# Attention and a maximum feed-forward on one core: the running maximum spread another way, the weights converted earlier, the first key sums on TensorE

## The chip, the cores and the metric

The kernel runs on one core of a Trainium2 chip. The metric is device time in microseconds (us), lower is better: three runs of the kernel before and their median, and one profiled execution with its own time. TensorE (PE) multiplies, VectorE (DVE) and ScalarE (ACT) work on SBUF and PSUM, GpSimd (POOL) on SBUF, and SyncE (SP) issues transfers. Each engine takes its instructions in order from its own queue and waits on semaphores for the others.

## The reference

Attention over 8 batches and 8 heads, 1152 keys, head size 64, with each two neighbouring queries averaged (576 queries), then a feed-forward in which a maximum over three products stands for the activation. All data is float32.

```python
q_pool = q.reshape(B, H, S // 2, 2, D).mean(axis=3)
scores = np.matmul(q_pool, k.transpose(0, 1, 3, 2)) / np.sqrt(D)
scores = scores - np.max(scores, axis=-1, keepdims=True)
attn = np.exp(scores)
attn = attn / (np.sum(attn, axis=-1, keepdims=True) + 1e-09)
x = np.matmul(attn, v).transpose(0, 2, 1, 3).reshape(B * 576, 512)
h = np.maximum(np.maximum(x @ w1, x @ w2), x @ w3)      # 768 wide
out = h @ w_out                                         # 4608 x 512
```

The weights w1, w2, w3 and w_out come as 64-bit floats.

## The kernel before, in words

**Units.** The attention is cut into 64 units, numbered d: one pair of heads of a batch and one half (288) of its queries; eight units make a batch. A unit's scores lie with the 128 keys of a block on the partitions and 2 x 288 columns (two heads), for nine blocks. `scores` makes them, `values` the rest.

- For each block PE multiplies with q split into a high and a low part (lines 542, 543, reduced float32: `F32R`), ACT copies the result out of PSUM into s (548), and DVE keeps the running maximum over the blocks in acc (554 for the first two, 557). Three blocks share one buffer "third" of `spool`, which has six: the copies of a unit wait for values and key sums of the unit two before it.
- acc still has 128 partitions to be reduced. PE transposes it in five pieces of 115 or 116 columns, three into one PSUM bank and two into another (593), DVE takes the maximum over each row (599), and PE spreads it back over all partitions by five more transposes of a broadcast operand (609). DVE subtracts it from the three thirds, in two spans of 345 and 231 columns (624), ACT takes the exponential (630).
- The sum over keys: POOL adds the nine blocks into ksum (643, 645), eight additions a unit. For units below `EARLY` = 16, PE turns ksum into columns with six one-column products (704), DVE adds EPS and inverts (714, 694), PE spreads it (719) and DVE multiplies (728). From unit 16, PE sums with a matrix of ones (687), ACT adds EPS (691), DVE inverts 288 columns (694), POOL multiplies (697).
- The value product: 18 products of 288 columns in float32 (673), two heads in two 64-wide tiles of the array; ACT copies it out (682), ACT and POOL split it into a high and a low part for the feed-forward (772, 775).

**Feed-forward.** Tokens go in nine chunks (512 each, then 448 and 576); chunk b starts when the attention of batch b is ready. 18 groups of weights (`NG`), each split into high and low, are multiplied (935), the maximum over three is formed (954, 956), split again (963, 966) and multiplied by the output weight (990). A chunk of weights is fetched from a scratch copy w_split in device memory (895).

**Conversion.** In chunk 0 each of the 18 groups, and the six tiles of the output weight, is converted from the bits of 64-bit floats (`convert`, 813 to 890): ACT rescales the high word into PSUM (835), DVE shifts (838), puts in the sign (843), isolates the power (848) and scales the low word (851), ACT takes the high part (862), and POOL (even tiles) or DVE (odd tiles, in halves of 256) subtracts (865) and adds (868). The product of chunk 0 reads the converted tile directly, and it is stored to w_split too (881). A tile is loaded when the tile two before it is done.

**Order.** Every operation is a `Step` with the engines it may run on, an assumed cost, and its predecessors. `arrange` (193) plays the steps through with these costs and, at each moment, gives an engine the ready step of lowest rank; a rank is the unit's number plus a constant of its kind (`RANK`) and for the first units a `NUDGE`. The resulting order is written out as the instruction order of the five engines. The bank pool "ff" of two PSUM banks serves the feed-forward, the sums, the conversions and, below unit 8, the value products.

Of the kernel before, what the change touches and what calls it, by code (L numbers as in the profile page):

```python
# [18 lines left out]
P = 128  # L19
# [4 lines left out]
CB = 115  # L24
DM = 512
# [11 lines left out]
    "qk": -364.0396,  # L37
    "cp": -126.5549,
    "mx": -318.2574,
    "rows": -969.9796,  # L40
    "red": -172.0313,
    "bc": -345.8464,
    "sub": 215.1752,
    "exp": 196.9402,
    "keys": -671.9276,
    "av": 14.8431,
    "xcopy": -516.1778,
    "psum": 398.4083,
    "eps": 343.2889,
    "inv": 357.0576,  # L50
    "xm": -706.0274,
    "load": 386.6538,
    "prep": 638.9001,
    "move": 1290.4425,
    "split": 283.1141,
    "ffn": -33.8173,
    "rate": 1.047,
    "mm": 49.0387,
    "fetch": 603.0832,
    "evac": -724.5554,  # L60
    "hhigh": 1228.3483,
    "hlow": -714.7034,
    "conv": 648.8915,
    "rate0": 4.5084,
    "first_qk": -97.1625,
    "first_cp": -630.79,
    "first_mx": 212.4188,
    "first_sub": 204.5779,
    "first_exp": 244.1512,
    "first_keys": -1118.9276,  # L70
    "first_av": 141.406,
    "first_xcopy": -152.0387,
    "first_psum": 65.359,
    "first_inv": 141.5566,
    "first_xm": 829.3378,
    "first_load": -197.5173,
    "first_prep": 180.1798,
    "first_move": -1436.3679,
    "first_split": 375.0794,
# [226 lines left out]
def tile_attention_ffn(  # L306
# [498 lines left out]
    def ffn(b, d):  # L805
# [108 lines left out]
        for g in range(4):  # L914
            supply(g)
# [159 lines left out]
```

## Time and profile before

| | |
|---|---|
| three runs | 1474.91, 1472.44, 1477.5 us; median 1474.91 |
| profiled execution | 1472.96 us, of which the span from the first to the last instruction is 1471.1 |
| mean granted TensorE clock | 0.978 |
| instructions | PE 8704, DVE 1441, ACT 1464, POOL 835 |
| transferred | 240.71 MB, mean 164 GB/s |

The page of the profile has the busy time of each engine, the span in 40 slices of 36.8 us (a digit is the busy share in tenths; PEclk is the granted TensorE clock in tenths), the DMA queues, the chain of waits that ended last, and the costliest groups of instructions by line. Other views: windows (busy time of each engine in stretches of the span, with instruction counts in brackets), lines (groups by line and shape: busy time, mean ns of one, then the idle time of the engine before them and what ended it), waits, and the timeline. A matmul's duration overlaps those of its neighbours, so a row of many gives less time than the sum of their durations.

### The profile page before, as it was taken

The numbers are of one execution on the slowest core, as the hardware profiler recorded it, in microseconds if no ns is written. First come the engines' busy times: TensorE is split into PE (matmuls) and PEld (weight loads), VectorE is DVE, ScalarE is ACT, GpSimd is POOL, SyncE is SP. The second block draws the span as 40 slices with busy tenths as digits, with TensorE's granted clock in tenths as the row PEclk, the third lists the DMA queues.
The fourth block names the chain that finished last, engine by engine and source line by source line (L and its number), as shares of the span: only waits on it lengthen the run. The fifth ranks groups of instructions, "written<-read, shape, count | busy, mean of one in ns | idle before, by whom it ended". The sixth has DMA issues, their size and how long they took to land.

```text
span 1471.1 us, 24704 instructions
## 1 busy us (share of the span) xinstructions
PE 1398.0 (95%) x8704; PEld 1098.5 (75%) x8704; DVE 1044.0 (71%) x1441; ACT 902.5 (61%) x1464; POOL 1079.1 (73%) x835
## 2 busy tenths in 40 slices
PE   4888999898899999999999999999999999999999
PEld 4566677675677878777777777777777777878999
DVE  3897789898877767777688778777787768861110
ACT  3776776567666666567566766666766757651211
POOL 1897975889868878679888878888787978772210
PEclk9988999998899999999999999999999999999999
DMA  6675456576456656565567556664566556414441
GB/s 181 169 203 147 122 153 207 184 206 194 118 151 185 201 155 182 168 181 148 148 192 203 152 145 191 182 182 134 163 189 184 149 148 185 144 69 162 149 161 59
DMA packets 114762, 240.71 MB, mean 164 GB/s; under 512 B 15440, under 2 KB 75216, under 8 KB 114640
## 3 DMA queue, kind: packets, MB, share of 16 engines
q1 hardware_dynamic: 114064, 238.55, 55.8%
q8 instruction: 70, 1.15, 0.3%
q10 hardware_dynamic: 576, 0.59, 0.2%
q14 instruction: 52, 0.43, 0.1%
HBM read 144.70 MB, written 18.87 MB: 111 GB/s over the span
## 4 chain that ended last, share of the span: by engine, by line
PE 75%; DVE 10%; DMA 4%; ACT 4%; issue 4%; POOL 2%; SPq 1%; ACTq 0%; DVEq 0%; POOLq 0%
PE ph L935 28%; PE pav L673 14%; PE po L990 10%; PE pqk L542 9%; PE pqk L543 8%; DVE s L624 3%; DVE acc L557 3%; DMA kraw<-in_kT_dram 2%; PE pmt L593 2%; PE psum L687 2%; PE pmb L609 2%; POOL ksum L645 1%; ACT s L548 1%; DVE w L848 1%; DVE w L843 1%
## 5 line engine op out<-in xcount | busy, mean ns | idle before, releaser
L645 POOL TENSOR_TENSOR ksum<-ksum,s 128x576 f32<-128x576 f32 x448 | 638.2, 1425 | 26.1 <-ACT s L630 3.5
L935 PE MATMUL ph<-xh,w 128*128 128x512 f32 (+2 forms) x1440 | 464.3, 376 | 2.7 <-DVE w L868 1.3
L548 ACT COPY s<-pqk 128x576 f32<-128x576 f32 x576 | 362.4, 639 | 103.4 <-PE pqk L543 97.8
L624 DVE TENSOR_TENSOR s<-s,pmb 128x693 f32<-128x693 f32 (+1 forms) x384 | 395.1, 1049 | 39.5 <-PE pmb L609 38.3
L542 PE MATMUL pqk<-qq,kc 128*128 128x288 f32 x1152 | 357.9, 326 | 56.1 <-DVE acc L557 30.7
L557 DVE TENSOR_TENSOR acc<-acc,pqk 128x576 f32<-128x576 f32 x448 | 335.3, 749 | 82.8 <-ACT s L548 78.1
L630 ACT ACTIVATE s<-s 128x693 f32<-128x693 f32 (+1 forms) x384 | 352.5, 933 | 41.9 <-DVE s L624 38.6
L543 PE MATMUL pqk<-qq,kc 128*128 128x288 f32 x1152 | 332.3, 303 | 0.0
L542 PEld LDWEIGHTS pqk<-qq,kc 128*128 128x128 f32 x1152 | 225.6, 196 | 113.7 <-DVE acc L557 44.5
L673 PE MATMUL pav<-s,v 128*64 128x288 f32 x2304 | 306.8, 418 | 1.3 <-ACT s L630 1.0
L935 PEld LDWEIGHTS ph<-xh,w 128*128 128x128 f32 x1440 | 263.1, 188 | 41.4 <-ACT xr L682 1.8
L935 PE MATMUL ph<-xl,w 128*128 128x512 f32 (+2 forms) x720 | 268.3, 373 | 0.0
L673 PEld LDWEIGHTS pav<-s,v 128*64 128x64 f32 x2304 | 165.2, 140 | 119.3 <-issue 16.6
L543 PEld LDWEIGHTS pqk<-qq,kc 128*128 128x128 f32 x1152 | 227.5, 197 | 10.4
L643 POOL TENSOR_TENSOR ksum<-s 128x576 f32<-128x576 f32 x64 | 92.0, 1437 | 107.8 <-ACT s L630 104.8
L956 DVE TENSOR_TENSOR hm<-hm,ph 128x512 f32<-128x512 f32 (+2 forms) x120 | 75.8, 631 | 126.8 <-PE ph L935 124.8
L966 POOL TENSOR_TENSOR h_lo<-hm,h_hi 128x512 fp32r<-128x512 f32 (+2 forms) x60 | 70.6, 1176 | 126.1 <-ACT h_hi L963 123.6
L935 PEld LDWEIGHTS ph<-xl,w 128*128 128x128 f32 x720 | 135.8, 189 | 11.5
L438 POOL TENSOR_TENSOR kraw<-kraw 128x1152 fp32r<-128x1152 f32 x31 | 82.8, 2670 | 63.1 <-DMA qraw<-in_qT_dram 26.6
L599 DVE TENSOR_REDUCE m<-pmt 116x3 f32<-116x384 f32 (+1 forms) x128 | 61.3, 488 | 89.9 <-PE pmt L593 89.8
L682 ACT COPY xr<-pav 128x288 f32<-128x288 f32 x64 | 25.5, 399 | 147.0 <-PE pav L673 146.9
L694 DVE RECIPROCAL rs<-rs 128x288 f32<-128x288 f32 (+1 forms) x64 | 96.5, 1507 | 17.7 <-ACT rs L691 17.3
(57 smaller groups left out, 1293.6 us busy)
## 6 DMA issues: line engine op xcount, KB each, us to landing
w<-w_split SPq DMA_DIRECT2D x144, 512.0 KB, 3.6
kc<-kraw SPq DMA_DIRECT2D x384, 96.0 KB, 2.2
qq<-qraw SPq DMA_DIRECT2D x252, 144.0 KB, 3.3
v<-in_vr_dram SPq DMA_DIRECT2D x32, 576.0 KB, 3.8
kraw<-in_kT_dram SPq DMA_DIRECT2D x31, 576.0 KB, 6.0
qraw<-in_qT_dram SPq DMA_DIRECT2D x31, 576.0 KB, 4.0
w<-in_win_dram SPq DMA_DIRECT2D x18, 512.0 KB, 5.9
w_split<-w SPq DMA_DIRECT2D x18, 512.0 KB, 5.5
```

What stands on the lines that cost most here:

```text
L542: nc.tensor.matmul(ps[:, h - hs[0], :QH], w, qq[:, 0, h], start=True, stop=False)
L543: nc.tensor.matmul(ps[:, h - hs[0], :QH], w, qq[:, 1, h], start=False, stop=True)
L548: nc.scalar.copy(o.s[kk // 3][:, kk % 3, slice(*hs)], o.ps[kk, hs][:, :, :QH])
L557: nc.vector.tensor_tensor(acc, acc, ps, op=ALU.max)
L624: nc.vector.tensor_tensor(s, s, o.pb[h][:, None, :w].broadcast_to([P, 3, w]), op=ALU.subtract)
L630: nc.scalar.activation(s, s, AF.Exp, scale=SCALE)
L643: vec[e].tensor_tensor(o.ksum, o.s[0][:, 0], x, op=ALU.add)
L645: vec[e].tensor_tensor(o.ksum, o.ksum, x, op=ALU.add)
L673: nc.tensor.matmul(o.pav[64 * h : 64 * h + 64, :QH], pr.v[:, kk, h], o.s[kk // 3][:, kk % 3, h], start=(kk == 0), stop=(kk == NK - 1),)
L694: nc.vector.reciprocal(o.rs, o.rs)
L935: nc.tensor.matmul(t.ps[:, : hi - lo], w[:, a, kk], xx[:, kk, lo:hi], start=(kk == 0 and i == 0), stop=(kk == 3 and i == 2),)
L990: nc.tensor.matmul(t.ps[:, : hi - lo], ww[:, kk, ms], hh[:, kk, lo:hi], start=(kk == 0 and i == 0), stop=(kk == 5 and i == 2),)
```

## The change

Five edits come together; the tables `RANK` and `NUDGE` have other numbers, and the order of all engines with them.

1. From unit 16 (`TURN`) the maximum goes another way. DVE reduces acc with a transposing reduction to 18 columns (`fold`), PE transposes that once (`turn`), DVE takes the maximum over four groups (`summit`: 18 x 32 values), ACT and DVE split it into a high and a low part (`m_high`, `m_low`), POOL multiplies it with a selecting pattern into a block-diagonal operand of 18 x 32 columns (`spread_out`), and PE multiplies ones by each half of it (`bcast_wide`, 288 columns in F32R). The spans are 288 and 288. The next unit's acc waits for `fold` alone.
2. In units 0 to 7 (`SUMS`) POOL adds no keys. After the values PE multiplies a 32-wide matrix of ones by all 18 half blocks, in four column tiles of the array (`columns_keys`); ACT copies the partial sums (`sums_copy`), PE adds and turns them (`sums_turn`).
3. `spool` has seven thirds, and in units 0 to 7 (`LENT`) the last third of a unit lies in one of four buffers that later hold h of the feed-forward.
4. A conversion uses whole tiles of 512: ACT rescales, DVE shifts and puts in the sign, ACT turns the low word into a float, POOL adds, ACT takes the high part, POOL subtracts. All 24 are put ahead of chunk 0, which fetches from w_split like the others.
5. `dynamic_dma_scratch_size=1024` is passed to the compiler.

```diff
+TURN = 16
+THIRDS = 7
+LENT = 8
+SUMS = 8
...
-    spool = ctx.enter_context(tc.tile_pool(name="spool", bufs=6))
+    spool = ctx.enter_context(tc.tile_pool(name="spool", bufs=THIRDS))
-    hpool = ctx.enter_context(tc.tile_pool(name="hpool", bufs=1))
+    hpool = ctx.enter_context(tc.tile_pool(name="hpool", bufs=4))
...
+        def fold(e):
+            nc.vector.tensor_reduce(
+                crest[d % 2][:, :NB],
+                o.acc.rearrange("p h q -> p (h q)").rearrange("p (t k) -> p t k", t=NB),
+                axis=AX.X, op=ALU.max, apply_transpose=True,
+            )
+        def turn(e):
+            o.pb[0] = ps_a.tile([P, 512], F32, tag="a", name=f"pmb{d}_0")
+            nc.tensor.transpose(o.pb[0][:, QH : QH + P], crest[d % 2], ident)
+        def summit(e):
+            o.top = o.pb[0][:NB, QH + P : QH + P + SQ]
+            nc.vector.tensor_reduce(
+                o.top, o.pb[0][:NB, QH : QH + P].rearrange("p (g k) -> p k g", g=4), axis=AX.X, op=ALU.max
+            )
+        def m_high(e):
+            nc.scalar.copy(parts2[d % 2][:NB], o.top)
+        def m_low(e):
+            nc.vector.tensor_tensor(parts2[d % 2][SQ : SQ + NB], o.top, parts2[d % 2][:NB], op=ALU.subtract)
+        def spread_out(e):
+            nc.gpsimd.tensor_tensor(
+                diag[d % 2][: 2 * SQ],
+                pick[:, :, None].broadcast_to([2 * SQ, NB, SQ]),
+                parts2[d % 2][:, None, :].broadcast_to([2 * SQ, NB, SQ]),
+                op=ALU.mult,
+            )
+            def bcast_wide(e, h=h):
+                if h:
+                    o.pb[h] = ps_b.tile([P, 512], F32, tag="b", name=f"pmb{d}_{h}")
+                half = diag[d % 2][:, NB // 2 * h : NB // 2 * h + NB // 2]
+                nc.tensor.matmul(o.pb[h][:, :QH], wide, half.rearrange("p t k -> p (t k)"), start=True, stop=True)
...
-        for kk in range(1, NK):
+        for kk in range(1, NK) if d >= SUMS else ():
...
+        def columns_keys(e):
+            o.psm = ps_ff.tile([P, 512], F32, tag="ff", name=f"psum{d}")
+            for kk in range(NK):
+                for h in range(2):
+                    t = 2 * h + kk % 2
+                    nc.tensor.matmul(
+                        o.psm[32 * t : 32 * t + 32, :QH], ones[:, :32], o.s[kk // 3][:, kk % 3, h],
+                        start=kk < 2, stop=kk >= NK - 2, tile_position=(0, 32 * t),
+                    )
+        def sums_copy(e):
+            nc.scalar.copy(o.kt, o.psm[:, :QH])
+        def sums_turn(e):
+            for i in range(3):
+                nc.tensor.matmul(
+                    o.psm[:96, QH + 2 * i : QH + 2 * i + 2], o.kt[:, 96 * i : 96 * i + 96], sel, start=True, stop=True
+                )
...
-                a = cstep([act(m)], rebias, [loaded] + gone, take="ff")
+                a = cstep([act(m)], rebias, [loaded], take="ff")
                 a = cstep([dve(m)], shift, [a])
-                a = cstep([dve(m)], sign, [a])
-                c = cstep([("act", 0.09 + m / 1200)], high, [a])
-                a = cstep([dve(m)], power, [a])
-                a = cstep([dve(m)], rest, [a], give=None if wide else "ff")
-                end = dve(m) if wide else pool(m)
-                c = cstep([end], low, [c, a])
-                return cstep([end], total, [c, a], give="ff" if wide else None)
+                a = cstep([dve(m)], sign, [a], give="ff")
+                c = cstep([act(m)], units_of, [loaded])
+                a = cstep([pool(m)], carry, [a, c])
+                c = cstep([("act", 0.09 + m / 1200)], high, [a] + gone + highs[-1:])
+                highs.append(c)
+                return cstep([pool(m)], low, [c, a])
...
         def supply(g):
-            if b:
-                fetch(g)
-            else:
-                convert(g)
-                fetched[g] = converted[g]
+            fetch(g)
...
+        if b == 0:
+            for g in range(NG + 6):
+                convert(g)
```

More of the change, by code (lines that the diff above doesn't have):

```diff
@@ L24 @@
 CB = 115
+SQ = 32
+NB = 18
+TURN = 16
 DM = 512
@@ L36 @@
 RANK = {
[L37 to L79, printed above, removed]
+    "qk": -1610.0615,
+    "cp": -180.1672,
+    "mx": -1253.2067,
+    "rows": -786.0194,
+    "turn": -1110.3828,
+    "top": 469.0602,
+    "diag": -189.5205,
+    "red": 77.8083,
+    "bc": -879.861,
+    "sub": 3840.475,
+    "exp": 984.6769,
+    "keys": -2399.561,
+    "av": 683.8571,
+    "xcopy": -1571.289,
+    "psum": 782.1931,
+    "eps": 214.1172,
+    "inv": 1557.6025,
+    "xm": -150.8782,
+    "load": -1024.6367,
+    "prep": 2386.9581,
+    "move": 1089.3258,
+    "split": -86.6507,
+    "ffn": 707.8881,
+    "rate": 5.1716,
+    "mm": 974.547,
+    "fetch": 157.873,
+    "evac": -1776.9799,
+    "hhigh": 675.1121,
+    "hlow": -1456.4392,
+    "conv": 1545.6563,
+    "rate0": 0.2612,
+    "first_qk": -105.5392,
+    "first_cp": 492.9138,
+    "first_mx": 996.4585,
+    "first_sub": 621.8249,
+    "first_exp": 463.1478,
+    "first_keys": -3171.6001,
+    "first_av": -465.3423,
+    "first_xcopy": 820.1949,
+    "first_psum": 3176.8613,
+    "first_inv": 117.4318,
+    "first_xm": -1228.9986,
+    "first_load": -1485.6615,
+    "first_prep": 53.3922,
+    "first_move": -618.3481,
+    "first_split": 1939.7866,
 }
 NUDGE = {
[81 rows of a table removed]
[90 rows of a table added]
 }
@@ L340, in tile_attention_ffn, with blank @@
     nc.vector.memset(eps, EPS)
+    sel = cpool.tile([P, 2], F32, name="sel")
+    nc.vector.tensor_tensor(sel, ident[:, ::64], ident[:, 32::64], op=ALU.add)
+    wide = cpool.tile([P, P], F32R, name="wide")
+    nc.vector.memset(wide.bitcast(F32), 1.0)
+    pick = cpool.tile([2 * SQ, NB], F32, name="pick")
+    crest = [cpool.tile([P, P], F32, name=f"crest{i}") for i in range(2)]
+    parts2 = [cpool.tile([2 * SQ, SQ], F32R, name=f"parts{i}") for i in range(2)]
+    diag = [cpool.tile([P, NB, SQ], F32R, name=f"diag{i}") for i in range(2)]
+    def blank():
+        for i in range(2):
+            rows = slice(SQ * i, SQ * i + SQ)
+            nc.vector.tensor_copy(pick[rows], ident[rows, SQ * i : SQ * i + NB])
+            nc.vector.memset(crest[i], 0.0)
+            nc.vector.memset(parts2[i].bitcast(F32), 0.0)
+            nc.vector.memset(diag[i].bitcast(F32), 0.0)
     wo_hi = cpool.tile([P, 6, DM], F32R, name="wo_hi")
@@ L515, in heads @@
         )
+    blanks = step("top", TURN - 4, [("dve", 3.2)], lambda e: blank(), [])
     units = {}
+    homes = [[], []]
     uses, last, finish, scaled, spreads = [[], []], [None], {}, {}, {}
@@ L522, in scores @@
         o = units[d] = Job()
-        o.n, o.half = n, half
+        o.n, o.half, o.d = n, half, d
         pr = pairs[n]
@@ L546, in copy @@
                     if kk % 3 == 0:
-                        o.s[kk // 3] = spool.tile([P, 3, 2, QH], F32, tag="s", name=f"s{d}_{kk // 3}")
+                        if d < LENT and kk == 6:
+                            s = hpool.tile([P, 3, NQ], F32, tag="t", name=f"s{d}_2")
+                            o.s[2] = s.rearrange("p k (h q) -> p k h q", h=2)
+                        else:
+                            o.s[kk // 3] = spool.tile([P, 3, 2, QH], F32, tag="s", name=f"s{d}_{kk // 3}")
                     nc.scalar.copy(o.s[kk // 3][:, kk % 3, slice(*hs)], o.ps[kk, hs][:, :, :QH])
@@ L571, in scores @@
                 after = [m]
-                if kk % 3 == 0 and old2:
-                    after += [old2.avs[kk + 2], old2.sums[kk + 1]]
+                if kk % 3 == 0:
+                    lent = d < LENT and kk == 6
+                    seq = homes[lent]
+                    past = len(seq) - (4 if lent else THIRDS)
+                    if past >= 0:
+                        was, last_kk = seq[past]
+                        after += [was.avs[last_kk], was.sums[last_kk - 1] if was.sums else chain[was.d]]
+                    seq.append((o, kk + 2))
                 c = x = step("cp", r, [act(n * QH)], copy, after + copies[-1:])
@@ L576, in scores @@
                 if kk:
-                    after = [c] + ([copies[0]] + (old.rows if old else []) if kk == 1 else [tops[-1]])
+                    after = [c] + ([copies[0]] + (old.accread if old else []) if kk == 1 else [tops[-1]])
                     x = step("mx", r, [dve(n * QH)], top, after, give="ff" if apart else None)
@@ L585, in scores @@
         pools = (ps_a, ps_b)
-        for h, (x0, x1) in enumerate([(0, 3 * CB), (3 * CB, 2 * QH)]):
+        late = d >= TURN
+        spans = [(0, QH), (QH, 2 * QH)] if late else [(0, 3 * CB), (3 * CB, 2 * QH)]
+        free_a = old.subs[0] if old else []
+        bc = {}
+        def fold(e):
+            nc.vector.tensor_reduce(
+                crest[d % 2][:, :NB],
+                o.acc.rearrange("p h q -> p (h q)").rearrange("p (t k) -> p t k", t=NB),
+                axis=AX.X,
+                op=ALU.max,
+                apply_transpose=True,
+            )
[18 more added lines that the diff above has]
+            )
+        if late:
+            x = step("red", d, [("dve", 0.775)], fold, [tops[-1], blanks, getattr(old2, "turned", None)])
+            o.accread = [x]
+            x = o.turned = step("turn", d, [pe(150)], turn, [x] + free_a)
+            x = step("top", d, [("dve", 0.25)], summit, [x])
+            y = step("top", d, [("act", 0.2)], m_high, [x] + getattr(old2, "full", []))
+            x = step("top", d, [("dve", 0.17)], m_low, [x, y] + getattr(old2, "full", []))
+            full = step("diag", d, [("pool", 1.16)], spread_out, [x, y] + getattr(old2, "bcs", []))
+            o.full = [full]
+            o.bcs = []
+        for h, (x0, x1) in enumerate(spans):
             nb, w = 3 - h, x1 - x0
@@ L613, in bcast @@
                     )
-            gone = xout[d - 1] if d > SPLIT and h else None
-            x = step("rows", d + 0.1 * h, [pe(133 * nb)], rows, [tops[-1], gone] + (old.subs[h] if old else []))
-            o.rows.append(x)
-            x = step("red", d, [("dve", 0.067 + nb * 0.133)], reduce, [x])
-            b = step("bc", d + 0.1 * h, [pe(89 + 99 * nb)], bcast, [x])
+            def bcast_wide(e, h=h):
[3 more added lines that the diff above has]
+                nc.tensor.matmul(
+                    o.pb[h][:, :QH], wide, half.rearrange("p t k -> p (t k)"), start=True, stop=True
+                )
+            gone = xout[d - 1] if d > SPLIT and h else None
+            if late:
+                b = step("bc", d + 0.1 * h, [pe(145)], bcast_wide, [full, gone] + (old.subs[1] if h else []), cols=QH)
+                o.bcs.append(b)
+            else:
+                x = step(
+                    "rows", d + 0.1 * h, [pe(133 * nb)], rows, [tops[-1], gone] + (old.subs[h] if old else [])
+                )
+                o.rows.append(x)
+                x = step("red", d, [("dve", 0.067 + nb * 0.133)], reduce, [x])
+                b = step("bc", d + 0.1 * h, [pe(89 + 99 * nb)], bcast, [x])
             for i in range(3):
@@ L635, in scores @@
                 o.exps[i, h] = step("exp", r, [("act", 0.109 + w / 400)], exp, [x])
+        if not late:
+            o.accread = o.rows
         o.sums = []
-        for kk in range(1, NK):
+        for kk in range(1, NK) if d >= SUMS else ():
             def key(e, kk=kk):
@@ L710, in columns @@
                     )
+        def columns_keys(e):
[4 more added lines that the diff above has]
+                    nc.tensor.matmul(
+                        o.psm[32 * t : 32 * t + 32, :QH],
+                        ones[:, :32],
+                        o.s[kk // 3][:, kk % 3, h],
+                        start=kk < 2,
+                        stop=kk >= NK - 2,
+                        tile_position=(0, 32 * t),
+                    )
+        def sums_copy(e):
+            o.kt = small.tile([P, QH], F32, tag="kt", name=f"kt{d}", bufs=1)
+            nc.scalar.copy(o.kt, o.psm[:, :QH])
+        def sums_turn(e):
+            for i in range(3):
+                nc.tensor.matmul(
+                    o.psm[:96, QH + 2 * i : QH + 2 * i + 2], o.kt[:, 96 * i : 96 * i + 96], sel, start=True, stop=True
+                )
         def add_eps6(e):
@@ L750, in values @@
         if early:
-            t = chain[d] = step("psum", d, [pe(1020)], columns, [o.sums[-1], a], cols=100, mode=1, take="ff")
+            if d < SUMS:
+                t = chain[d] = step("keys", d, [pe(2300)], columns_keys, [a], cols=5184, mode=2, take="ff")
+                t = step("eps", d, [("act", 0.4)], sums_copy, [t])
+                t = step("psum", d, [pe(300)], sums_turn, [t], cols=10, mode=1)
+            else:
+                t = chain[d] = step("psum", d, [pe(1020)], columns, [o.sums[-1], a], cols=100, mode=1, take="ff")
             t = step("inv", d, [("dve", 0.1)], add_eps6, [t, spreads.get(d - 2)])
@@ L803, in tile_attention_ffn @@
     converted, stored = {}, {}
+    highs = []
     def ffn(b, d):
@@ L820, in load @@
                 nc.sync.dma_start(o.w.rearrange("p n t -> p (n t)"), dram.bitcast(U32))
-            wide = j % 2 == 1
-            m = DM // 2 if wide else DM
+            m = DM
             def part(x):
@@ L855, in high, with carry @@
+                def carry(e):
+                    nc.gpsimd.tensor_tensor(o.f, o.f, o.low, op=ALU.add)
                 def high(e):
                     if j < NG:
-                        if j not in wt:
-                            wt[j] = wpool.tile([P, 2, NPAIR, P], F32R, tag="w", name=f"w{b}_{j}")
-                        o.hi, o.lo = (wt[j][:, i].rearrange("p c m -> p (c m)") for i in range(2))
+                        o.t = wpool.tile([P, 2, NPAIR, P], F32R, tag="w", name=f"wc{j}")
+                        o.hi, o.lo = (o.t[:, i].rearrange("p c m -> p (c m)") for i in range(2))
@@ L860, in high @@
                     else:
                         o.hi, o.lo = wo_hi[:, j - NG], wo_lo[:, j - NG]
-                    nc.scalar.copy(o.hi[:, cut], q.ff)
+                    nc.scalar.copy(o.hi[:, cut], o.ff)
                 def low(e):
-                    vec[e].tensor_tensor(q.ff, q.ff, o.hi[:, cut], op=ALU.subtract)
-                def total(e):
-                    vec[e].tensor_tensor(o.lo[:, cut], q.ff, q.low.bitcast(F32), op=ALU.add)
-                a = cstep([act(m)], rebias, [loaded] + gone, take="ff")
+                    nc.gpsimd.tensor_tensor(o.lo[:, cut], o.ff, o.hi[:, cut], op=ALU.subtract)
@@ L895, in load @@
                 nc.sync.dma_start(wt[g].rearrange("p a c m -> p (a c m)").bitcast(F32), wscr[g].bitcast(F32))
-            fetched[g] = [ffn_step("fetch", at, 24 * g, [("sp", 0.4)], load, wuse[base + g - 4] + [stored[g]], size=512)]
+            fetched[g] = [ffn_step("fetch", at, 24 * g, [("sp", 0.4)], load, (wuse[base + g - 4] if base + g >= 4 else [stored[NG - 4 + g], highs[NG - 1]]) + [stored[g]], size=512)]
         def needed(kk, lo, hi):
@@ L902, in begin @@
         def begin():
-            h.hi = hpool.tile([P, 6, NQ], F32R, tag="h_hi", name=f"h_hi{b}")
-            h.lo = hpool.tile([P, 6, NQ], F32R, tag="h_lo", name=f"h_lo{b}")
+            third = lambda name: hpool.tile([P, 3, NQ], F32, tag="t", name=f"{name}{b}").bitcast(F32R)
+            quarters = [third(f"h{i}") for i in range(4)]
+            h.hi, h.lo = quarters[:2], quarters[2:]
         def supply(g):
-            if b:
-                fetch(g)
-            else:
+            fetch(g)
+        base = NG * b
+        if b == 0:
+            for g in range(NG + 6):
                 convert(g)
-                fetched[g] = converted[g]
-        base = NG * b
         for g in range(4):
@@ L971, in ffn @@
                         hdone += [x, y]
-                wuse.append([tail[0]] + ([] if b else [stored[g]]))
+                wuse.append([tail[0]])
                 if g + 4 < NG:
@@ L975, in ffn @@
         if b == 0:
-            for g in range(NG, NG + 6):
-                convert(g)
             hdone += [c for i in range(NG, NG + 6) for c in converted[i]]
```

36 lines of the change are left out of this document (17 added, 19 removed), and 171 rows, old and new, of the table NUDGE.

## The prediction

> **What bounds the kernel now.** I read the page first (busy shares, the 40 slices, the chain), then a table of windows cut where the slices change character, then the groups with shapes kept apart, and last the timeline of TensorE around one maximum.
>
> ```profile
> span 1471.1 us, 24704 instructions
> PE 1398.0 (95%) x8704; PEld 1098.5 (75%) x8704; DVE 1044.0 (71%) x1441; ACT 902.5 (61%) x1464; POOL 1079.1 (73%) x835
> ...
> PE   4888999898899999999999999999999999999999
> ...
> PEclk9988999998899999999999999999999999999999
> ...
> PE 75%; DVE 10%; DMA 4%; ACT 4%; issue 4%; POOL 2%; SPq 1%; ACTq 0%; DVEq 0%; POOLq 0%
> ```
>
> TensorE is busy 95% of the span and holds 75% of the chain; what is left open lies in the first eleven slices, which are also those with a granted clock below 9. A row of the answer on line 935 gives the place at which the feed-forward begins, and the windows cut there:
>
> ```profile
> L935 PE MATMUL ph<-xh,w x1440: 290/392/628, 191.8 to 1448.4; 128*128 128x512 f32 x126, 128*128 128x288 f32 x36, 128*128 128x448 f32 x18
> ```
>
> ```profile
> core 0: us, PE busy (x) PEld busy (x) DVE busy (x) ACT busy (x) POOL busy (x), PEclk, DMA share, GB/s
> 0.00:13.00 13.00, 0.00 (x0) 0.01 (x1) 2.54 (x8) 3.12 (x6) 0.70 (x6) 1.00 0.77 206
> 13.00:191.80 178.80, 152.95 (x1008) 112.11 (x1009) 139.12 (x218) 122.50 (x190) 140.92 (x100) 0.91 0.59 161
> 191.80:404.80 213.00, 189.51 (x1195) 142.16 (x1195) 195.62 (x345) 144.88 (x246) 170.32 (x131) 0.93 0.59 178
> 404.80:1325.00 920.20, 912.75 (x5609) 707.92 (x5604) 686.45 (x835) 605.34 (x965) 739.61 (x569) 1.00 0.58 165
> 1325.00:1471.10 146.10, 142.77 (x900) 136.25 (x898) 20.32 (x37) 26.68 (x60) 27.58 (x31) 1.00 0.39 134
> ```
>
> Four stages. A, 13 to 191.8: attention alone, no engine over 86% of its time, clock 0.91. B, 191.8 to 404.8: attention with feed-forward chunk 0, DVE busy 195.6 of 213 (92%), PE idle 23.5 us at clock 0.93: DVE sets the pace. C, 404.8 to 1325: PE idle 7.45 us of 920 at clock 1.00: PE is the bound, and the feed-forward fills its gaps. D, the tail: feed-forward alone, PE idle 3.3 of 146. So from 404.8 on, time is TensorE work; before it, time is waiting.
>
> **The change, part by part: the maximum from unit 16.** Per unit, five transposes of the running maximum and five that spread it go; one transpose and two 288-column products come.
>
> ```profile
> 830.04 0.29 PE L543 MATMUL pqk<-qq,kc 128*128 128x288 f32 x1
> 830.17 0.38 PE L593 MATMUL pmt<-ident,acc 128*116 128x128 f32 x2
> 830.31 0.38 PE L542 MATMUL pqk<-qq,kc 128*128 128x288 f32 x1
> 830.53 0.29 PE L543 MATMUL pqk<-qq,kc 128*128 128x288 f32 x1
> 830.66 0.29 PE L542 MATMUL pqk<-qq,kc 128*128 128x288 f32 x1
> 830.79 0.29 PE L543 MATMUL pqk<-qq,kc 128*128 128x288 f32 x1
> 830.92 0.46 PE L609 MATMUL pmb<-ident,m 116*128 116x116 f32 x3
> 831.15 0.39 PE L542 MATMUL pqk<-qq,kc 128*128 128x288 f32 x1
> 831.38 0.30 PE L543 MATMUL pqk<-qq,kc 128*128 128x288 f32 x1
> ```
>
> Columns are start, length, engine, line. Durations overlap, so I price by starts. Score products follow each other at 0.13 us (830.53, 830.66, 830.79). From 830.04 to 830.53 there are two such steps (0.26) and two transposes: 0.49, so 0.115 each. From 830.79 to 831.38: 0.59 less 0.26 is 0.33 for three, 0.11 each. Ten cost 1.12 us. The new ones: one transpose 0.115, and two products in the shape of line 542's, 0.13 each: 0.375, or 0.40 with something for three more interruptions. Saved 0.72 us a unit, 48 units (16 to 63): **34.5 us**, all of it where PE is the bound. Bounds: 0.55 if each new product pays 0.1 more for standing alone (830.92 and 831.15 show the neighbours stretched from 0.29 to 0.39), 0.9 if the old groups cost more elsewhere: 26 to 43.
>
> What it adds on the other engines, none of which is the bound in C:
>
> ```profile
> L599 DVE TENSOR_REDUCE m<-pmt 116x3 f32<-116x384 f32 x64 | 35.6, 556 | 83.7 <-PE pmt L593 83.6
> L599 DVE TENSOR_REDUCE m<-pmt 116x2 f32<-116x256 f32 x64 | 26.9, 420 | 6.2 <-PE pmt L593 6.2
> L714 DVE TENSOR_SCALAR rs<-psum 96x6 f32<-96x6 f32 x16 | 2.4, 152 | 1.8 <-PE psum L704 1.7
> L431 POOL TENSOR_TENSOR qraw<-qraw 128x576 fp32r<-128x576 f32 x31 | 44.3, 1430 | 8.8 <-ACT qraw L427 8.6
> L682 ACT COPY xr<-pav 128x288 f32<-128x288 f32 x64 | 25.5, 399 | 147.0 <-PE pav L673 146.9
> ```
>
> The two reductions give 1.06 ns per element ((556-420)/128). The folding reduction reads 576 elements: 0.76 us by that slope, no row shows one that transposes, so 0.76 to 1.5. The second reduction (128 elements) 0.28, the subtraction 0.15 to 0.2: DVE 1.2 us in place of 0.98. ACT gets a copy of 32 elements, under the 0.40 of 288. POOL's product has 576 elements out in fp32r, like line 431: 1.43, and 2.9 if two spread operands halve its rate; I take 1.43, the same size and type. Over the 46 units in C that is 10 us on DVE (686 to 696) and 66 on POOL (740 to 806, 91% of some 886).
>
> The path from the last maximum to the first subtraction grows:
>
> ```profile
> 829.26 0.54 PE L593 MATMUL pmt<-ident,acc 128*116 128x128 f32 x3
> 831.42 1.23 DVE L624 TENSOR_TENSOR s<-s,pmb 128x1035 f32<-128x1035 f32 x1 [0.41 <-PE pmb L609]
> ```
>
> Now it takes 2.16 us (829.26 to 831.42). After: 0.76 + 0.3 + 0.28 + 0.2 + 0.2 + 1.43 + 0.3 of work, 3.5, and six hand-overs for three, an estimate of 4.4 us. What hides it is the feed-forward and the next unit's scores on PE. On POOL the product queues behind key sums; behind it wait the next key sums. On DVE the subtractions, on PE whatever stands behind the first spreading product. Uncovered, 2.3 us times 48 would be 110 us; in C the present path costs PE almost nothing, so I take 5 us (0 to 20).
>
> **Conversions and key sums in the first stages.**
>
> ```profile
> 13.00:191.80 178.80, 0.00 (x0) 0.16 (x1) 15.50 (x32) 5.80 (x12) 4.72 (x4) 0.91 0.59 161
> 191.80:404.80 213.00, 56.64 (x216) 38.45 (x216) 72.23 (x160) 29.05 (x60) 23.50 (x20) 0.93 0.59 178
> ```
>
> These are the same windows for tile w alone: the conversions take 72.2 us of DVE and 29.1 of ACT in stage B. There they disappear: all 24 tiles are to be done before chunk 0 begins, because it now fetches from the split copy in memory. Then B's DVE load is 195.6 - 72.2 = 123.4, ACT 115.8, POOL 146.8 and PE 189.5 at clock 0.93, which is 176 at full clock: PE becomes the bound of B. With C's idle share (7.45/920) B takes 177.5 in place of 213: **35.5 us less**. Bounds: 12 if only half the idle goes and the clock stays, 43 if part of the busy time is waiting inside matmuls.
>
> Stage A has to take them in.
>
> ```profile
> L835 ACT ACTIVATE w<-w 128x512 f32<-128x512 f32 x12 | 7.8, 652 | 6.7 <-DVE hm L956 4.5 <-DMA w<-in_wout_dram 1.4 <-DMA w<-in_win_dram 0.7
> L862 ACT CAST w<-w 128x512 fp32r<-128x512 f32 x9 | 6.1, 676 | 4.5 <-DVE w L843 4.4
> L838 DVE TENSOR_SCALAR w<-w 128x512 uint32<-128x512 uint32 x12 | 8.2, 687 | 2.5 <-ACT w L835 2.2
> L843 DVE SCALAR_TENSOR_TENSOR w<-w,w 128x512 uint32<-128x512 uint32 x12 | 8.2, 684 | 0.1
> L865 POOL TENSOR_TENSOR w<-w,w 128x512 f32<-128x512 f32 x9 | 11.7, 1305 | 2.3 <-ACT w L862 2.3
> L645 POOL TENSOR_TENSOR ksum<-ksum,s 128x576 f32<-128x576 f32 x448 | 638.2, 1425 | 26.1 <-ACT s L630 3.5
> L704 PE MATMUL psum<-ones,ksum 128*96 128x1 f32 x192 | 18.1, 221 | 3.6 <-POOL ksum L645 2.2 <-DVE wo_lo L868 1.2 <-DVE w L851 0.2
> ```
>
> A tile now costs DVE two passes, 0.687 + 0.684 = 1.37, so 24 take 32.9; ACT 2 x 0.652 + 0.676 = 1.98, 47.5; POOL two at 1.305, 62.6. DVE in A: 139.1 - 15.5 + 32.9 = 156.5 of 178.8 (88%). ACT: 122.5 - 5.8 + 47.5, and 0.4 a unit for the copy of the sums, 167 (94%). POOL loses 8 x 8 key additions of 1.425, 91.2: 140.9 - 4.7 - 91.2 + 62.6 = 108. PE gains the key sums:
>
> ```profile
> 944.78 4.58 PE L673 MATMUL pav<-s,v 128*64 128x288 f32 x36
> 949.29 0.54 PE L593 MATMUL pmt<-ident,acc 128*116 128x128 f32 x3
> ```
>
> One unit's value product takes 4.51 us of PE (944.78 to 949.29), with two 64-wide tiles side by side. The key sums stream the same 18 blocks of 288 columns through four 32-wide tiles: 2.26 if four overlap twice as well as two, 4.5 if no better. I take 2.3, as the tiles are only narrower, plus 0.3 for turning the sums, less 0.56 for six one-column products (18.1/192 each): 2.0 a unit, 16 in all, and PE in A goes to 169 of 178.8 at clock 0.91. The Trainium skill, "TensorE: Matmul & The Clock Gate", section "Measured speedup vs the span model", gives 2.38 for three column tiles, not 3; by that the key sums would be an estimate of 2.85 us, 4 us more in all. No run here shows it.
>
> So in A three engines stand near 90% at its present length, and weight loads and stores come on top of a DMA share of 0.59. The SP queue issues them in order among the loads of q, k and v. Three more things help: third score blocks in the four buffers of h and a seventh score buffer (a unit's scores no longer wait for the unit two before it), key sums that finish right behind the values, and slack in the six tiles of the output weight, which chunk 0 needs last. B's best share for a bound engine is DVE's 92%; ACT's 167 at 92% is 181.5, and the filling of a chain through ACT, DVE, ACT, POOL adds some: I take **A 10 us longer** (10 shorter to 36 longer, the last when ACT reaches only 78%, 167/0.78 = 214).
>
> Other edits (split maximum halves at 288 instead of 345 and 231, blank tiles set once, smaller DMA scratch) move no engine total by over 4 us.
>
> **Sum.** The profiled execution took 1472.96 (span 1471.1 and 1.9 around it): 1473 - 34.5 - 35.5 + 10 + 5 = 1418. The median of the runs lies 1.95 above that execution: **1420**.
>
> **The rivals.** (1) Only half of it pays: ACT and the transfers hold A at 78%, 36 us longer, or POOL at 91% of C sets the pace and the saved PE work turns to idle. First: 1420 + 26 = 1446; second: 1420 + 34.5 = 1454.5. For it speak the 0.59 DMA share and 94% of ACT, against it the slack of POOL in C.
>
> (2) Slower: the new maximum stalls PE. In order engines wait on each other five times more, and PE stands before the spreading product while POOL works off a key sum (1.43) and the product (1.43). With 2.9 us lost in each of 48 units, 139 us in place of 5: 1420 + 134 = 1554. It is slower than before from (1475 - 1420 + 5)/48 = 1.25 us a unit. For it:
>
> ```profile
> DVE s L624 <- PE pmb L609: 38.3, 32, 3.1
> ```
>
> the subtraction waits for the spread already, 32 times, 1.2 us each. Against it: PE had feed-forward work to put there and idled 7.45 us in C.
>
> (3) Better: A gets shorter by 10 (more score buffers) and B and C give their upper bounds, 43 each: 1420 - 20 - 7.5 - 8.5 = 1384.
>
> (4) No change: A 36 longer (+26 against the forecast), stalls at 20 (+15), B at its lower bound of 12 (+23.5), C at 26 (+8.5) would be 1493; with B at a middle 24 (+11.5) and C as forecast it is 1420 + 26 + 15 + 11.5, about 1473.
>
> **How the numbers follow.** Forecast 0.55 (1395 to 1442), rival 1 0.18 (1443 to 1462), rival 3 0.12 (1375 to 1394), no change 0.03, slower 0.12. The range 1385 to 1462 leaves out rival 2, rival 4 and the better half of rival 3. A measurement of this kernel tells 0.3%, 4.4 us: faster 0.85, same 0.03, slower 0.12.
>
> **What would show it.** Right: the transposes of lines 593 and 609 left at 80 instructions each (16 units); about 0.4 us of PE a unit for the new spread; no conversion on any engine after chunk 0 begins; PE idle from there under 2%, at clock 1.00; POOL near 90% in the middle. Wrong: chunk 0 beginning after 215; PE waits behind the product on POOL of over 1 us a unit; key sums of 4 us; a folding reduction over 1.5 us.

## The result, and the profile after

The changed kernel takes 1425.3 us (median of four runs, 1423.15 to 1428.05) beside 1473.68 for the kernel before on the same chip: a ratio of 0.967, 95% interval 0.9643 to 0.9697. It is faster by 48 us; 1420 was forecast. The profiled execution took 1425.01, its span is 1423.2. First its page: busy shares, two rows of the slices, the chain by engine.

```profile
span 1423.2 us, 24396 instructions
...
PE 1365.0 (96%) x8608; PEld 1063.3 (75%) x8608; DVE 1001.9 (70%) x1355; ACT 915.3 (64%) x1520; POOL 1069.1 (75%) x843
...
PE   4878889999999999999999999999999999999999
...
PEclk9999889999999999999999999999999999999999
...
PE 85%; DVE 4%; ACT 3%; DMA 3%; issue 2%; POOL 2%; SPq 1%; ACTq 0%; POOLq 0%; DVEq 0%
```

TensorE is busy for 90% or more of every slice from the 7th on, where it was from the 12th, and its share of the chain went from 75% to 85%. Its busy time fell by 33.0 us and its idle time by 14.9: the kernel works less and waits less. To compare stages of the same meaning I cut both traces where feed-forward chunk 0 starts, where chunk 1 starts, and where chunk 6 ends. The windows of the kernel before (its stage A is in the prediction):

```profile
191.80:424.30 232.50, 209.01 (x1306) 158.39 (x1305) 209.88 (x363) 158.15 (x267) 180.95 (x138) 0.93 0.59 176
424.30:1332.10 907.80, 900.35 (x5526) 697.44 (x5525) 672.18 (x818) 593.06 (x947) 733.10 (x565) 1.00 0.57 164
1332.10:1471.10 139.00, 135.67 (x869) 130.51 (x868) 20.32 (x37) 25.70 (x58) 23.45 (x27) 1.00 0.41 139
```

And after (stretch and length, then PE, PEld, DVE, ACT, POOL with instruction counts, clock, DMA share, GB/s):

```profile
12.60:205.30 192.70, 160.88 (x1170) 109.79 (x1171) 143.18 (x213) 147.63 (x234) 81.76 (x65) 0.91 0.75 224
205.30:384.30 179.00, 176.98 (x1197) 138.60 (x1197) 127.30 (x190) 122.38 (x195) 151.02 (x114) 0.99 0.61 177
384.30:1279.30 895.00, 886.43 (x5334) 681.58 (x5333) 703.34 (x898) 613.99 (x1026) 801.82 (x626) 1.00 0.60 171
1279.30:1423.20 143.90, 140.76 (x910) 133.33 (x908) 22.73 (x39) 27.96 (x62) 33.78 (x35) 1.00 0.40 134
```

Chunk 0 starts 13.5 us later (205.3 for 191.8). From there to the end it is 1217.9 us for 1279.3: 61.4 less. The stages after the first do not hold the same attention units, so their lengths are not compared one by one. Two starts do enclose nearly the same work, those of chunks 2 and 6 (30.8 and 30.9 units by their score products, four chunks of feed-forward); before, then after:

```profile
567.80:1190.20 622.40, 616.81 (x3807) 477.06 (x3805) 469.83 (x572) 414.66 (x664) 510.31 (x392) 1.00 0.60 171
```

```profile
535.20:1140.00 604.80, 597.53 (x3599) 458.81 (x3597) 476.37 (x608) 417.87 (x696) 548.83 (x427) 1.00 0.61 176
```

That is 17.6 us, 0.57 a unit; at this rate 48 units give 27.4. The other 34.0 of the 61.4 are a remainder and are put down to the time of chunk 0. What the windows show fits: PE's idle time there went from 23.5 us to 2.0, and the clock from 0.93 to 0.99, by which the old 209.0 us of busy time would shrink by 12.7, an estimate; 21.5 and 12.7 make 34.2. So: +13.5, -34.0, -27.4, together -47.9.

The conversions have left chunk 0's time for the most part and not wholly. The part of tile w there:

```profile
205.30:384.30 179.00, 59.47 (x216) 38.05 (x217) 6.88 (x10) 9.76 (x15) 11.74 (x10) 0.99 0.61 177
```

Ten passes on DVE are five tiles of the 24. Their 6.88 us of DVE stand beside 72.2 before.

What the new operations take, from the lines with shapes kept apart (busy, mean ns):

```profile
L638 DVE TRANSPOSE_TENSOR_REDUCE crest<-acc 128x18 f32<-128x576 f32 x48 | 37.1, 772 | 0.7
L652 DVE TENSOR_REDUCE pmb<-pmb 18x32 f32<-18x128 f32 x48 | 13.5, 282 | 12.0 <-PE pmb L648 11.6
L663 POOL TENSOR_TENSOR diag<-pick,parts 64x576 fp32r<-64x576 f32 x48 | 55.3, 1152 | 0.0
L828 PE MATMUL psum<-s,ones 128*32 128x288 f32 x288 | 21.0, 409 | 0.5 <-ACT xr L793 0.5
```

The folding reduction (0.77) and the second one (0.28) came as worked out from the old reductions' slope; POOL's product is cheaper than taken (1.15 for 1.43). The key sums are dearer: 21.0/8 = 2.6 us of busy time a unit, and 2.55 from their start to that of the next product, in each of the eight units, for 2.3.

And the path of one maximum, unit 40, from the timeline:

```profile
812.20 0.75 DVE L597 TENSOR_TENSOR acc<-acc,pqk 128x576 f32<-128x576 f32 x1
813.83 0.77 DVE L638 TRANSPOSE_TENSOR_REDUCE crest<-acc 128x18 f32<-128x576 f32 x1
814.92 0.27 PE L648 MATMUL pmb<-ident,crest 128*128 128x128 f32 x1
815.23 0.29 DVE L652 TENSOR_REDUCE pmb<-pmb 18x32 f32<-18x128 f32 x1 [0.63 <-PE pmb L648]
816.70 0.16 ACT L657 CAST parts<-pmb 18x32 fp32r<-18x32 f32 x1
816.85 1.46 POOL L756 TENSOR_TENSOR ksum<-ksum,s 128x576 f32<-128x576 f32 x1
817.24 0.18 DVE L660 TENSOR_TENSOR parts<-pmb,parts 18x32 fp32r<-18x32 f32 x1
818.21 1.15 POOL L663 TENSOR_TENSOR diag<-pick,parts 64x576 fp32r<-64x576 f32 x1
821.28 0.43 PE L714 MATMUL pmb<-diag,wide 128*128 128x288 f32 x2
822.38 1.05 DVE L733 TENSOR_TENSOR s<-s,pmb 128x864 f32<-128x864 f32 x1
```

From the end of the last maximum (812.95) to the first subtraction it takes 9.4 us, of which about 3.3 are the steps themselves. The rest is queueing: the copy on ACT starts 1.2 us after the reduction before it, POOL's product stands behind the key sum of 816.85, the spread comes 1.9 us after the product, behind other products in PE's order. Averaged over units 16 to 63 (ends and starts of these two lines in the trace) this path went from 5.7 us to 10.2; counted as the prediction counts it, from the start of the first transpose or of the folding reduction, from 3.7 to 9.7.

### The profile page after: what moved, and what is told of

Read it like the earlier page. It is cut to its first block, busy times and chain, and to the rows that moved or that the text cites. A ratio compares the mean times of both kernels' runs of the same rounds, so it can differ in the third digit from the quotient of the medians.

```text
span 1423.2 us, 24396 instructions
## 1 busy us (share of the span) xinstructions
PE 1365.0 (96%) x8608; PEld 1063.3 (75%) x8608; DVE 1001.9 (70%) x1355; ACT 915.3 (64%) x1520; POOL 1069.1 (75%) x843
## 4 chain that ended last, share of the span: by engine, by line
PE 85%; DVE 4%; ACT 3%; DMA 3%; issue 2%; POOL 2%; SPq 1%; ACTq 0%; POOLq 0%; DVEq 0%
PE ph L1068 30%; PE pav L784 19%; PE pqk L578 11%; PE po L1123 10%; PE pqk L579 9%; DVE acc L597 2%; PE psum L798 2%; ACT s L588 1%; DVE s L733 1%; PE pmb L714 1%; DMA w<-in_win_dram 1%; PE psum L828 1%; ACT s L739 1%; POOL ksum L756 1%; DMA qq<-qraw 1%
## 5 line engine op out<-in xcount | busy, mean ns | idle before, releaser
L756 POOL TENSOR_TENSOR ksum<-ksum,s 128x576 f32<-128x576 f32 x392 | 557.9, 1423 | 20.9 <-ACT s L739 2.5
L733 DVE TENSOR_TENSOR s<-s,pmb 128x864 f32<-128x864 f32 (+2 forms) x384 | 395.5, 1045 | 41.6 <-PE pmb L714 36.3
L578 PE MATMUL pqk<-qq,kc 128*128 128x288 f32 x1152 | 346.0, 317 | 49.7 <-DVE acc L597 20.4
L739 ACT ACTIVATE s<-s 128x864 f32<-128x864 f32 (+2 forms) x384 | 353.7, 932 | 53.6 <-DVE s L733 51.4
L579 PE MATMUL pqk<-qq,kc 128*128 128x288 f32 x1152 | 327.6, 301 | 0.0
L578 PEld LDWEIGHTS pqk<-qq,kc 128*128 128x128 f32 x1152 | 222.8, 193 | 121.4 <-issue 37.1
L579 PEld LDWEIGHTS pqk<-qq,kc 128*128 128x128 f32 x1152 | 224.4, 195 | 11.6
L1099 POOL TENSOR_TENSOR h<-hm,h 128x512 fp32r<-128x512 f32 (+2 forms) x60 | 70.9, 1181 | 98.7 <-ACT h L1096 98.5
L1123 PE MATMUL po<-h,wo_hi 128*128 128x512 f32 (+2 forms) x480 | 139.2, 374 | 0.2 <-ACT ob L1139 0.2
L754 POOL TENSOR_TENSOR ksum<-s 128x576 f32<-128x576 f32 x56 | 80.7, 1441 | 69.7 <-ACT s L739 69.6
L805 DVE RECIPROCAL rs<-rs 128x288 f32<-128x288 f32 (+1 forms) x64 | 96.5, 1507 | 23.4 <-ACT rs L802 21.5
```

What stands on the lines that cost most here:

```text
L578: nc.tensor.matmul(ps[:, h - hs[0], :QH], w, qq[:, 0, h], start=True, stop=False)
L579: nc.tensor.matmul(ps[:, h - hs[0], :QH], w, qq[:, 1, h], start=False, stop=True)
L733: nc.vector.tensor_tensor(s, s, o.pb[h][:, None, :w].broadcast_to([P, 3, w]), op=ALU.subtract)
L739: nc.scalar.activation(s, s, AF.Exp, scale=SCALE)
L756: vec[e].tensor_tensor(o.ksum, o.ksum, x, op=ALU.add)
L805: nc.vector.reciprocal(o.rs, o.rs)
```

## The experiments

The first theory: three terms, +13.5 (conversions and key sums taken into stage A), -34 (conversions gone from chunk 0's time), -27 (TensorE work of the maximum). Against it: the order of the queues makes the gain, or the buffers do. Each run is compared with the 1425.3 of the changed kernel, or with the kernel before on its own chip (1473.65 to 1475.05). In every run the orders of all queues are laid out anew for its steps, so an edit moves the order too. The smaller DMA scratch, the fifth edit of the change, was not run alone.

### The old maximum in all units

```diff
-TURN = 16
+TURN = 64
```

> The changed kernel with the maximum by ten transposes in all 64 units. Theory (the new path saves TensorE work where TensorE is the bound, 17.6 us over the 31 units between the starts of chunks 2 and 6, so 0.57 a unit): 48 units give 27 us back, 1452 us (1446 to 1460), with the stretch between those two starts near 622 us again. Rival (the gain from unit 16 on comes from the order of the queues or from the earlier release of the running maximum): within 6 us of 1425.

1472.21 us (ratio to before 0.999, 0.9976 to 1.0003), 47 more. Chunk 0's time is 182.8 us (179.0 in the changed kernel); the loss lies behind it:

```profile
385.40:1329.90 944.50, 923.98 (x5702) 714.18 (x5702) 691.42 (x852) 617.47 (x983) 759.80 (x586) 1.00 0.56 162
```

PE's busy time over the whole span is 1398.7 for 1365.0: 33.7 us, 0.70 a unit, close to the 0.72 of the prediction. Ten more come as idle time of PE (20.5 in this window for 8.6). The work is confirmed and the rival is not, but the total lies above the theory's 1446 to 1460: undoing the part costs more than the part. That an order fitted to the other path leaves the gaps is a guess which this run does not test.

### Key sums on POOL in all units

```diff
-SUMS = 8
+SUMS = 0
```

> The changed kernel with the key sums on GpSimd in all units. Theory (stage A is held by ScalarE and the chain through it, GpSimd had slack there): GpSimd gets 91 us back on 82 us of 193, 90% busy, TensorE loses 21 us of work; stage A 0 to 15 us longer, 1425 to 1440. Rival 1 (GpSimd was what held the first units): stage A over 20 us longer, 1446 or more. Rival 2 (TensorE is what holds them now): stage A 10 us shorter, 1415.

1455.24 us, 30 more, and the loss lies in stage A: chunk 0 starts at 236.3 in place of 205.3, and the stretch from chunk 2 to chunk 6 is the same to 0.1 us.

```profile
12.40:236.30 223.90, 168.54 (x999) 120.80 (x999) 147.54 (x217) 148.49 (x232) 176.75 (x133) 0.82 0.64 194
```

The first rival's value came: 95 us more on POOL make stage A 31 us longer. Its total does not explain that, for POOL is busy 176.75 of 223.9, 79%; each conversion needs it twice, between steps on ACT and DVE, which this run does not take apart. The clock falls to 0.82.

### Six score buffers, none lent; six and lent; seven, none lent

```diff
-THIRDS = 7
+THIRDS = 6
-LENT = 8
+LENT = 0
```

> The changed kernel with six score buffers in all units, none lent. Theory (the buffers let stage A carry the conversions at the same unit period): stage A 10 to 20 us longer, 1435 to 1446, TensorE from chunk 0 on as now. Rival (engines are full there and the buffers bring nothing): within 5 us of 1425.

1487.7 us, 62 more and slower than before (1.0091, 1.0066 to 1.0116). But stage A is no longer than in the changed kernel (189.0 us for 192.7). PE is idle 44.8 us between chunk 1's start and chunk 6's end. Theory and rival both missed: the buffers matter, and not where I had put them. So the two edits were taken apart. Six in the pool, four lent:

```diff
-THIRDS = 7
+THIRDS = 6
```

> The changed kernel with six score buffers in the pool, and the four of h still lent in units 0 to 7. Theory after the first runs (the seventh buffer covers the longer path of the maximum from unit 16 on, the lent ones change little): stage A within 8 us of 193, TensorE idle 35 to 45 us between the start of chunk 1 and the end of chunk 6, 1475 to 1490. Rival (the lent buffers carried the loss of the run with neither): 1425 to 1435.

1487.13 us (1.0093, 1.0059 to 1.0127), in the theory's range. Stage A 188.5, and then:

```profile
385.40:1336.20 950.80, 908.66 (x5293) 690.93 (x5292) 703.91 (x888) 614.77 (x1020) 791.41 (x617) 0.97 0.56 161
```

Idle 42.1 us (950.80 less 908.66). The waits show at what PE stands, first here, then in the changed kernel's window from chunk 1's start to chunk 6's end:

```profile
PE pqk L578 <- DVE acc L597: 25.2, 35, 1.8
```

```profile
PE pqk L578 <- DVE acc L597: 2.4, 4, 0.8
```

It is mostly the score products that wait, for DVE's running maximum, which frees their PSUM buffers; the spreading products hardly wait for POOL's product (1.3 us here, 0.4 there). DVE in turn stands at the maximum's own steps: its second reduction and its subtractions wait for PE 112.3 us here and 42.7 there. Seven in the pool, none lent:

```diff
-LENT = 8
+LENT = 0
```

> The changed kernel with seven score buffers and none lent. Theory (as for the run with six and the lent ones): stage A within 8 us of 193, the rest as the changed kernel, 1420 to 1433. Rival (the lent buffers matter in the first eight units): stage A 15 us longer or more, 1440 and above.

1422.64 us (ratio 0.9649, 0.9631 to 0.9667; stage A 189.2, idle 7.9 in stage C). The lent buffers bring nothing; the seventh buffer is worth 62 us to this kernel, and the loss without it lies from unit 16 on. The path of the maximum is no longer with six buffers (8.7 us on average for 10.2); what is missing is the room to run ahead. With the old maximum six are enough: the run of the tables alone, below, idles 7.8 us from chunk 1 to chunk 6. The changed kernel with six buffers and the old maximum was not run. This is the fastest kernel of the study, though its interval overlaps that of the changed one.

### The new maximum alone, and with the seventh buffer

The kernel before, with its own tables and, of the other edits, only the smaller DMA scratch (cut; the steps are those of the change):

```diff
+TURN = 16
...
+            x = step("red", d, [("dve", 0.775)], fold, [tops[-1], blanks, getattr(old2, "turned", None)])
...
-    "red": -172.0313,
+    "turn": -969.9796, "top": -172.0313, "diag": -172.0313,
+    "red": -172.0313,
```

> The kernel before with its own tables, and the new maximum from unit 16 as the only change (six score buffers; the new steps take the ranks of the old transposes and reductions). Theory (27 us of TensorE work saved, the path of 10 us in place of 6 uncovered with six buffers): TensorE idle 35 us or more from chunk 1 to chunk 6, 1475 to 1495, so no gain. Rival (the path is hidden by the feed-forward whatever the buffers): 1447, idle under 15.

1488.13 us, slower than before (1.0092, 1.0071 to 1.0114) and in the theory's range, with less idle in stage C than the 35 it named: 24.9.

```profile
190.60:436.30 245.70, 217.59 (x1294) 164.58 (x1293) 215.88 (x372) 160.64 (x275) 187.09 (x143) 0.89 0.57 169
436.30:1336.90 900.60, 875.73 (x5111) 673.34 (x5110) 663.57 (x840) 583.44 (x970) 755.24 (x590) 0.98 0.56 165
```

Columns nine and on are PE's clock, DMA share and rate. The mean clock of the whole run is 0.956, it was 0.978: PE is busy 1393 us, 5 less than before, with 27 to 34 us less to do.

The same with a seventh buffer, as against the run above (cut):

```diff
+THIRDS = 7
...
-    spool = ctx.enter_context(tc.tile_pool(name="spool", bufs=6))
+    spool = ctx.enter_context(tc.tile_pool(name="spool", bufs=THIRDS))
...
```

> The kernel before with its own tables, the new maximum from unit 16 and a seventh score buffer. Theory (the seventh buffer covers the path): TensorE idle under 20 us from chunk 1 to chunk 6, 1447 (1438 to 1460). Rival (only tables fitted to the new path cover it): idle 35 us or more, 1475 and above.

1487.22 us (1.01, 1.0064 to 1.0136); the profiled execution is the slowest of the four, 1496.76. The total is the rival's. From chunk 1 on the theory holds: PE idles 13.5 of 853 us, at clock 1.00. The time is lost before: chunk 0 starts at 214.5 and chunk 1 at 497.6, with 35.2 and 43.6 us idle and clocks of 0.88 and 0.90. With the old tables, old conversions and a seventh buffer the queues of the first units come out worse; why was not followed further.

### The tables

The kernel before with the changed kernel's `RANK` and `NUDGE` and nothing else:

```diff
 RANK = {
-    "qk": -364.0396,
+    "qk": -1610.0615,
...
```

> The kernel before with the rank and nudge tables of the changed kernel and nothing else. Theory (the work moved and removed makes the gain): within 15 us of 1474, either side. Rival (the order made the gain): 1450 or less.

1494.04 us, 1.4% slower than before (1.0112 to 1.0167). That is 20 us more, outside the theory's 15 and far from the rival: the tables alone make no gain. From chunk 1 to chunk 6, with six buffers and the old maximum, PE idles 7.8 us, as before (7.5):

```profile
435.40:1349.40 914.00, 906.23 (x5612) 705.06 (x5612) 681.07 (x834) 605.09 (x964) 745.83 (x575) 1.00 0.57 165
```

The loss lies in chunk 0's time, where PE idles 32.1 us at clock 0.89 (190.2 to 435.4).

And the changed kernel with the tables of before (new steps ranked as above):

```diff
 RANK = {
-    "qk": -1610.0615,
+    "qk": -364.0396,
...
```

> The changed kernel with the rank and nudge tables of the kernel before (the new steps take the ranks of the old transposes and reductions). Theory (the work moved makes the gain, the tables cover the longer path and the conversions' place): 1430 to 1455. Rival 1 (the order matters little): 1420 to 1429. Rival 2 (without its own tables the change gains nothing): 1465 or more.

1501.99 us, 77 more and slower than before (1.0174 to 1.0225): the second rival. Chunk 0 starts at 215.6, PE idles 14.4 us in chunk 0's time and 35.0 behind it, with a mean clock of 0.966. The work that the change removes is removed here too; all of its worth goes into gaps and into the lower clock, at which PE is busy 1402 us.

### The old conversion

The changed kernel with the four passes on DVE, the split tiles read directly, during chunk 0 (cut to the place of the conversion):

```diff
...
-        if b == 0:
-            for g in range(NG + 6):
-                convert(g)
+            if b:
+                fetch(g)
+            else:
+                convert(g)
+                fetched[g] = converted[g]
...
```

> The changed kernel with the old conversion (four passes on VectorE and more, during chunk 0), all else as changed. Theory (the early conversion costs stage A 10 to 13 us and saves stage B some 34): stage A 180, VectorE over 88% busy and TensorE idle 20 us or more in stage B, 1447 (1440 to 1465). Rival (the seventh buffer and the moved key sums would fill stage B anyway): 1420 to 1432.

1477.2 us (1.0026, 1.0008 to 1.0044), 52 more.

```profile
13.10:195.70 182.60, 159.62 (x1166) 110.77 (x1167) 129.27 (x203) 117.02 (x185) 39.37 (x28) 0.92 0.54 147
195.70:458.40 262.70, 231.51 (x1439) 174.38 (x1438) 231.29 (x396) 178.12 (x299) 210.44 (x160) 0.93 0.58 170
```

As the theory says: stage A 10 us shorter, DVE busy 231.3 of 262.7 (88%), PE idle 31.2 at clock 0.93. The buffers and the moved key sums do not fill chunk 0's time; the old conversions are what slows it. The total is above the theory's range, again with more idle behind (14.3 for 8.6).

### POOL's product twice

```diff
         def spread_out(e):
-            nc.gpsimd.tensor_tensor(
+            for _ in range(2):
+                nc.gpsimd.tensor_tensor(
...
-            full = step("diag", d, [("pool", 1.16)], spread_out, [x, y] + getattr(old2, "bcs", []))
+            full = step("diag", d, [("pool", 2.32)], spread_out, [x, y] + getattr(old2, "bcs", []))
```

> The changed kernel with GpSimd's product from unit 16 issued twice (the same values written again, 1.15 us more on GpSimd and on the path of the maximum). Theory (GpSimd at 802 of 895 us has slack and the seventh buffer covers the path): 1425 to 1434, TensorE idle under 20 us in stage C. Rival (GpSimd at 95% sets the pace of stage C): 1445 or more, idle over 30.

1455.9 us, 31 more: the rival's time, with slightly less idle than its 30.

```profile
385.60:1309.20 923.60, 894.49 (x5331) 685.27 (x5330) 700.39 (x894) 615.69 (x1024) 852.90 (x669) 0.99 0.57 166
```

PE idles 29.1 us. POOL is at 92% here and at 90% in the changed kernel. Whether its load or the 1.15 us more on the path does it, this run does not separate.

### The new maximum from unit 8

```diff
-TURN = 16
+TURN = 8
-LENT = 8
+LENT = 0
```

> The changed kernel with the new maximum from unit 8 instead of 16, and no lent buffers (which brought nothing). Theory (TensorE is the bound of stage B now, idle 2 us of 179): eight more units save 0.57 us each, 1418 against 1422.6 without the lent buffers (1413 to 1421). Rival (the longer path is not covered while the first chunk is worked off): 1423 to 1440.

1433.09 us (0.9726, 0.9705 to 0.9748), 10 more than with unit 16 and none lent: the rival's value. PE idles 4.6 us in chunk 0's time and 22.6 behind it, for 2.1 and 7.9. The rival named the first; most of the loss is in the second. The earlier start saves work (PE is busy 1361.9 us for 1364.6) and loses more in idle time; why was not followed.

## Why the prediction was right, point by point

- **TensorE work of the maximum: right.** 0.72 us a unit was predicted, less 5 us of stalls, 29.5 in all. Nearly equal work gives 27.4, carried from 31 units to 48; the run with the old maximum shows 0.70 a unit in busy time.
- **What covers the longer path: wrong.** The prediction let the path grow by 2.3 us and named the feed-forward and the next unit's scores as cover. Its 2.16 us before was one short case; the mean, counted the same way, is 3.7, and it grew by 6.0, mostly by queueing. The cover is the seventh score buffer, which the prediction put down to stage A. With six, PE idles 42 us and the change is a loss. That the change carried the buffer is luck for the 5 us of stalls in the sum. The slower rival had the danger right and the place wrong: the part alone is 13 us slower than before, but PE stands mostly at the next score products, behind a DVE held up by the maximum, and hardly at the spreading one.
- **POOL's slack at 91%: wrong** in what it was to mean. The load came as worked out (90%), but 1.15 us more a unit, on POOL and on the path at once, cost 31 us.
- **Chunk 0's time: right.** 35.5 was predicted; the remainder is 34.0, and the old conversion brings DVE's 88% and PE's idle time back. Not as said: five of the 24 tiles are still converted after chunk 0 begins, where all were to be done before.
- **Stage A: right in size, not in cause, and so in part by luck.** 10 us longer was predicted from ACT at 94%, with 24 conversions. Chunk 0 starts 13.5 later, but stage A then holds 19 conversions and 10.0 units of scores, where it held 10.6, and ACT is busy 147.6 of 192.7 (77%), DVE 74%, PE 83%, POOL 42%. No engine's total bounds it. Key sums on POOL make it 31 us longer, conversions taken out make it 10 shorter; what chain holds it beyond that stays open. The transfers, which the first rival named, rose from a share of 0.59 to 0.75, and no run tests them. The lent buffers were given a part in it and have none.
- **Key sums: 2.55 us for 2.3**, counted from start to start as the value product's 4.51 was: four tiles gain 1.8 times on two, not quite twice. By the Trainium skill's rate of 2.38 for three tiles ("TensorE: Matmul & The Clock Gate", section "Measured speedup vs the span model") the prediction had an estimate of 2.85; the measured value lies between.
- **The order: not priced.** The prediction treated the tables as part of the change without a cost of their own. Taken back one at a time, the maximum, the key sums, the seventh buffer, the conversion and the tables cost 47, 30, 62, 52 and 77 us, 268 together for a gain of 48. The terms add up only in the kernel with all of them and its own order.

## What to carry to other kernels

Where one engine is the bound, price a change by the work it takes from that engine at the spacing of its neighbours, and then look for the buffer that lets the others run ahead: a longer path costs nothing only as far as buffers reach. Do not count an engine at 90% that others wait on as having slack: here one operation more a unit cost 31 us. Where the order of all queues is laid out ahead, a part tried alone in the old order can lose although its work is saved: judge it by busy time, idle time and clock, not by the total alone.

## What the runs showed of the hardware

- Where TensorE waits more, more than the wait is lost. With six buffers, four lent, stage C is 55.8 us longer than in the changed kernel (950.8 for 895.0), of which 33.6 are idle time (42.1 for 8.6); the granted clock fell from 1.00 to 0.97 and the busy time rose by 22, with slightly fewer instructions. The trace's record of the clock stands at half for 54.6 us of that stage, for 3.4 in the changed kernel, though no gap of PE there is longer than 2.2 us. The clock is lower with the key sums on POOL too: 0.82 in stage A for 0.91.
- POOL's product with two operands spread by a stride of zero takes 1.15 us for 576 columns on 64 partitions, where the plain two-operand ones of 576 columns on 128 partitions take 1.42 to 1.44. Whether the stride, the partitions or the operation makes the difference was not run.
- A reduction on DVE that transposes on the way costs what a plain one would by the slope of two others: 0.77 us for 576 elements, 0.76 by the slope.
